# Attention with clustered masks and two feed-forward layers: the first two heads in another order, two heads assigned as a pair, a second bank for transpositions

## The chip, the cores and the metric

One core of a Trainium2 chip runs the whole program. The metric is device time in microseconds (us) of one execution; less is better. The core has a matrix engine (TensorE, PE below; PEld is its loading of weights), a vector engine (VectorE, DVE), an engine for functions of one input (ScalarE, ACT), GpSimd (POOL) and SyncE (SP), which here only issues DMAs. Each engine works through its instructions in order; semaphores hold an instruction until what it needs from another engine is there. PE writes to PSUM, eight banks, from which DVE and ACT read.

## The reference

Attention over 2 batches x 8 heads, 768 positions, 64 dimensions, with a mask: each query and each key is assigned to the nearest of 16 centroids of its head (largest cosine), and a query sees the keys of its own cluster only. Then two feed-forward layers over the 1536 x 512 result.

```python
q_assign = argmax(einsum('bhsd,hcd->bhsc', q_n, c_n))      # k_assign alike
mask = q_assign[:, :, :, None] == k_assign[:, :, None, :]
scores = where(mask, scale * q @ k.T, -1e9)
attn = exp(scores - max(scores)); attn /= (sum(attn) + 1e-9)
x = (attn @ v) reshaped to [1536, 512]
h = x @ w_in;   x = (h * sigmoid(1.702 * h)) @ w_out        # 512 -> 2048 -> 512
g = x @ w_gate; out = (g * sigmoid(g) * (x @ w_val)) @ w_out2
```

All is float32.

## The kernel before, in words

The 16 heads (2 batches x 8) go one after the other. For a head h, the steps that matter here are:

- `hi_q`, `hi_k` (ACT) and `lo_q`, `lo_k` (DVE or POOL) split queries and keys into a rounded part and the difference. Results lie in `q2(h)` and `k2(h)`, five buffers each, used in turn; inputs come by DMA into four staging buffers (`load_qk`).
- `similar` (line 435): four matmuls of 128x384 give the products of keys and queries with the centroids, into one bank (`sims`). `largest` and `assign` (lines 459 to 504) turn them on DVE into rows that say to which cluster each position belongs: a transposition of 32x32 blocks, an addition, a maximum, a comparison, a weighting, a second maximum, a comparison, a scaling, and two transpositions back (`oT`). For one head these work on 192 columns and the rows are copied into `q2` and `k2` by given engines (line 494). For a pair they work on 384 columns; the first head's rows are copied (line 502), the second's go by DMA (line 504).
- `smax(h, c, n)` (lines 517, 522): a matmul of 128x384 with its own rounded parts, for block c of six and half n of two, and a reduction on DVE to the maximum of each query. Twelve of them, then `mneg` (line 533), then the row of negated maxima, brought into `q2` either by three matmuls and a copy per half (`mrow_at_once`, lines 540, 544) or by one matmul, a copy and a DMA (`mrow`, lines 549 to 552).
- `scores(h, c, n)` (lines 564, 571): two matmuls of 128x384 into one bank (`st`), the second with the cluster rows and the row of maxima, then an exponential on ACT into `p`. Twelve of them.
- `pv(h, c)` (line 580): six products of `p` with the values, six times; `norm` (lines 597 to 599) divides by the sum.
- `to_x` (lines 609 to 616): when a pair of heads is done, three transpositions on PE for each half n, a copy on ACT and a subtraction on DVE give the input of the feed-forward part.

Loops: the scores of head h stand with the maxima of head h + 1 between them; behind them the six products of head h, and among these the row of maxima and the splitting of later heads, and at odd h the assignment of heads h + 3 and h + 4 and `to_x` for the pair finished before. From head 3 on, steps that decode the feed-forward weights (lines 70 to 86) stand among the products too. The first heads have an order of their own, written out ahead of the loop: head 0's maxima stand with warming matmuls (`keep_warm`, line 353), the first half of its scores alone, the second with the first half of head 1's maxima; heads 1, 2 and 3 are assigned one by one, from head 4 on in pairs.

The order of the work is that of the code: the scheduler is told to leave every engine's instructions in the order in which they are written. Where two tiles share memory, a wait is put in. PSUM is in four pools: `ps_m` two banks (maxima), `ps_x` one bank (similarities, the row of `mrow`, transpositions of `to_x`, each third maximum), `ps_o` two banks (products, warming matmuls), `ps_s` three banks (scores, some similarities).

Of the kernel before, what the change touches and what calls it, by code (L numbers as in the profile page):

```python
# [8 lines left out]
F32 = mybir.dt.float32  # L9
# [16 lines left out]
def tile_cluster_attention_two_mlps(ctx: ExitStack, tc: tile.TileContext, qk, v, cen, w1, w2, wg, wv, w3, out):  # L26
    nc = tc.nc
# [6 lines left out]
    SC = S // 128  # L34
    HALF = S // 2
    NH = B * H
# [235 lines left out]
    with ExitStack() as att:  # L272
# [233 lines left out]
        def do(steps):  # L506
            for _ in steps:
                pass
# [94 lines left out]
        def to_x(hp, n):  # L603

            b, j = divmod(hp, H // 2)
            x = xr_t[hp]
            ps = ps_x.tile([128, HALF], F32, tag="x", name="xt")
            for c in range(SC // 2):
                nc.tensor.transpose(
                    out=ps[:, c * 128:(c + 1) * 128],  # L610
                    in_=x[:, n * (SC // 2) + c, :, :].rearrange("p a d -> p (a d)"),
                    identity=ident,
                )
            at = slice(n * HALF, (n + 1) * HALF)
            nc.scalar.copy(xh[b][:, j, at], ps)
            nc.vector.tensor_tensor(
                out=xl[b][:, j, at], in0=ps, in1=xh[b][:, j, at].bitcast(F32), op=ALU.subtract
            )
# [21 lines left out]
        lo_k(2, nc.gpsimd)  # L640
        extra_rows(3)
        load_qk(4)
        for i, (c, n) in enumerate((c, n) for m in range(2) for n in range(2) for c in range(3 * m, 3 * m + 3)):
            smax(0, c, n, *((ps_m, "m"), (ps_m, "m"), (ps_s, "s"), (ps_s, "s"), (ps_s, "s"))[i % 5])
            keep_warm(1)
            if i == 5:
                mneg(0, slice(0, SC // 2))
            if i == 9:
                mrow_at_once(0, 0, ps_o, "o")
        mneg(0, slice(SC // 2, SC))  # L650
        sims = similar([1])
        for c in range(SC):
            scores(0, c, 0)
        do(largest([1], sims))
        do(assign([1], (nc.vector.tensor_copy, nc.gpsimd.tensor_copy)))
        lo_q(2, nc.gpsimd)
        mrow_at_once(0, 1, ps_o, "o")
        maxima = list(steps)
        for i in range(SC):
            scores(0, i, 1)  # L660
            smax(1, *maxima[i], *((ps_m, "m"), (ps_m, "m"), (ps_x, "x"))[i % 3])
        hi_k(3)
        hi_q(3)
        lo_k(3, nc.gpsimd)
# [1 line left out]
        for t in v_t[1:]:  # L666
            nc.gpsimd.memset(t[:, :, D:D + 1], 1.0)
        extra_rows(4)

        for h in range(NH):
            more, ahead = h + 1 < NH, h + 4 < NH
            if h > 0:
                maxima = list(steps) if more else []
            for step in steps if h else ():
                scores(h, *step)
                if maxima:
                    next_smax(h + 1, maxima)
            if h == 0:  # L680
                load_qk(5)
            if ahead and h > 0:
                hi_q(h + 4)
            if 0 < h < NH - 1:
                mneg(h + 1)
            if h % 2 == 0 and 0 < h < NH - 3:
                do(assign([h + 2, h + 3]))
# [5 lines left out]
            for c in range(SC):  # L693
                pv(h, c)
                if more and c == 0:
                    if h > 0:
                        mrow(h + 1)
                    load_v(h + 1)
                    if ahead:
                        if h > 0:  # L700
                            hi_k(h + 4)
                            lo_q(h + 4)
                            lo_k(h + 4)
                        if h + 6 < NH:
                            load_qk(h + 6)
                        if h + 5 == NH:
                            qk1_stack.close()
                            stage_stack.close()
                            for to, t in zip((xh, xl), new_x(pool(ctx, "x1", 1, side="right"), 1)):
                                to.append(t)  # L710
                            w_pools.append(pool(ctx, "wd0", MID, side="right"))
                if h == 0:
                    if c == 0:
                        sims = similar([2])
                    if c < 3:
                        for i in (2 * c, 2 * c + 1):
                            smax(1, *maxima[SC + i], *((ps_m, "m"), (ps_s, "s"), (ps_m, "m"), (ps_s, "s"))[i % 4])
                    if c == 3:
                        mneg(1)
                        mrow(1, ps_o, "o")  # L720
                        hi_k(4)
                        hi_q(4)
                        do(largest([2], sims))
                        do(assign([2], (nc.scalar.copy, nc.vector.tensor_copy)))
                        lo_k(4)
                        lo_q(4)
                if h == 1 and c == 1:
                    do(largest([3], similar([3])))
                    do(assign([3]))
                if h > 0 and c == 0:  # L730
                    norm(h - 1)
                if h == NH - 1 and c > 0:
                    run([], [[("1", 0)], [("1", 1), ("2", 0)], [("1", 2)], [("2", 1)], []][c - 1], 0)
# [1 line left out]
                if h == 1 and c == 4:  # L735
                    fetch_to(2)
                if h % 2:
                    if c == 2 and ahead:
                        do(largest([h + 3, h + 4], similar([h + 3, h + 4], ps_s, "s")))
                    if c in (3, 4) and h > 2:  # L740
                        to_x((h - 3) // 2, c - 3)
# [74 lines left out]
```

## Time and profile before

| | |
|---|---|
| median of three runs | 855.67 us (855.47 to 855.67) |
| profiled execution | 855.47 us, span of the profile 853.5 us |
| PE busy | 837.7 us, 98% |
| DVE, ACT, POOL busy | 594.0, 432.9, 27.7 us |
| attention part | up to about 285 us |
| heads' scores begin | head 1: 38.97 us; head 2: 60.91 us; head 3: 77.02 us |

The profile is one execution, recorded by the chip. Busy time is time in which an engine works on an instruction; a matmul's duration includes its run through the array, so matmuls that follow each other overlap, and 0.34 us of duration come each 0.17 to 0.18 us. The time that an engine waits stands in brackets behind the instruction that ended the wait, with the instruction that released it. The clock column is the mean share of full speed that PE's clock was granted; 1.00 is 2.4 GHz, 0.50 is 1.2 GHz.

### The profile page before, as it was taken

Reading aid. Unit: us, or ns where it says so; the run is one execution under the profiler, and the core shown is the slowest. Engines: PE = TensorE matmul, PEld = TensorE weight load, DVE = VectorE, ACT = ScalarE, POOL = GpSimd, SP = SyncE. Lnnn points to the kernel's source line nnn. Section 1 sums busy time; section 2 is a strip of 40 time slices with the busy share of each in tenths; the row PEclk is TensorE's granted clock in tenths of the full one; section 3 lists DMA queues with packets and bytes.
Section 4 is the critical chain, followed back from the end, with each engine's and each line's share of the span. In section 5 each row is a group of like instructions: output and inputs, shape, how many; then the busy total and the mean of one; then the engine's idle time right before and its main releaser. Section 6 shows DMA issues by size and latency. Waiting matters only on the chain.

```text
span 853.5 us, 12841 instructions
## 1 busy us (share of the span) xinstructions
PE 837.7 (98%) x5034; PEld 752.4 (88%) x5034; DVE 594.0 (70%) x1147; ACT 432.9 (51%) x819; POOL 27.7 (3%) x43
## 2 busy tenths in 40 slices
PE   8899999999999999999999999999999999999998
PEld 6789999999999888888888888888888888888886
DVE  8788988988975488888877676787664344433433
ACT  6657667668565365565655454554432233322322
POOL 8400000000000000000000000000000000000000
PEclk9989999999999999999999999999999999999999
DMA  6121231230132033333222222222200010000001
GB/s 123 27 78 34 81 83 34 58 82 15 40 93 60 26 96 103 116 107 121 76 99 75 75 75 99 64 86 74 74 1 1 1 49 25 1 1 1 1 1 74
DMA packets 26191, 49.71 MB, mean 58 GB/s; under 512 B 14522, under 2 KB 14612, under 8 KB 26132
## 3 DMA queue, kind: packets, MB, share of 16 engines
q1 hardware_dynamic: 25188, 47.14, 18.8%
q10 hardware_dynamic: 944, 1.77, 0.6%
q8 instruction: 39, 0.64, 0.3%
q14 instruction: 20, 0.16, 0.1%
HBM read 45.12 MB, written 3.15 MB: 57 GB/s over the span
## 4 chain that ended last, share of the span: by engine, by line
PE 87%; DVE 9%; ACT 2%; issue 1%; DMA 1%; POOL 0%; SPq 0%; DVEq 0%; ACTq 0%; POOLq 0%
PE h L156 39%; PE a L156 27%; PE pv L580 9%; PE st L564 7%; PE smax L517 4%; DVE nm L522 1%; ACT q L321 1%; DVE q L330 1%; DVE k L336 1%; DVE T L462 1%; DVE T L459 1%; DVE T L472 1%; DVE mx L470 1%; DVE T L474 1%; DVE oT L491 1%
## 5 line engine op out<-in xcount | busy, mean ns | idle before, releaser
L156 PE MATMUL h<-xh,sp 128*128 128x512 f32 (+1 forms) x1280 | 327.2, 337 | 0.1
L156 PEld LDWEIGHTS h<-xh,sp 128*128 128x128 f32 x1280 | 223.2, 189 | 28.5 <-issue 0.3
L156 PE MATMUL h<-xl,sp 128*128 128x256 f32 (+1 forms) x640 | 215.9, 337 | 0.0
L188 DVE SCALAR_TENSOR_TENSOR t<-t,h 128x512 f32<-128x512 f32 x112 | 61.9, 553 | 160.8 <-ACT t L185 160.8
L185 ACT ACTIVATE t<-h 128x512 f32<-128x512 f32 x112 | 54.8, 489 | 204.1 <-PE h L156 204.1
L156 PE MATMUL a<-g,sp 128*128 128x512 f32 (+1 forms) x768 | 139.4, 337 | 0.0
L156 PEld LDWEIGHTS a<-g,sp 128*128 128x128 f32 x768 | 119.9, 189 | 16.7
L580 PEld LDWEIGHTS pv<-v,p 128*128 128x128 f32 x1152 | 134.3, 192 | 0.0
L580 PE MATMUL pv<-v,p 128*128 128x65 f32 x1152 | 134.0, 273 | 0.0
L156 PEld LDWEIGHTS h<-xl,sp 128*128 128x128 f32 x640 | 120.9, 189 | 14.3
L571 ACT ACTIVATE p<-st 128x384 f32<-128x384 f32 x192 | 90.7, 491 | 34.7 <-PE st L564 27.9
L522 DVE TENSOR_REDUCE nm<-smax 128x1 f32<-128x384 f32 x192 | 100.3, 556 | 9.8 <-PE smax L517 9.6
L156 PE MATMUL a<-sp,g 128*128 128x512 f32 x432 | 106.1, 390 | 0.0
L564 PE MATMUL st<-q,k 128*128 128x384 f32 (+1 forms) x384 | 100.5, 349 | 0.2 <-ACT q L544 0.2
L150 DVE TENSOR_TENSOR sp<-w,sp 128x512 fp32r<-128x512 f32 x136 | 92.9, 685 | 5.2 <-ACT sp L149 5.1
L156 PEld LDWEIGHTS a<-sp,g 128*128 128x128 f32 x432 | 79.5, 188 | 15.6
L149 ACT CAST sp<-w 128x512 fp32r<-128x512 f32 x136 | 83.2, 614 | 0.0
L197 DVE TENSOR_TENSOR g<-t,g 128x512 fp32r<-128x512 f32 x112 | 62.1, 554 | 16.1 <-ACT g L194 11.5
L564 PEld LDWEIGHTS st<-q,k 128*128 128x128 f32 (+1 forms) x384 | 70.1, 194 | 2.1 <-ACT p L571 0.6
L517 PE MATMUL smax<-k,q 80*128 80x384 f32 x192 | 66.6, 349 | 4.6 <-DVE nm L522 2.1
L194 ACT CAST g<-t 128x512 fp32r<-128x512 f32 (+1 forms) x48 | 24.8, 516 | 81.2 <-DVE t L193 81.2
L190 ACT CAST g<-t 128x512 fp32r<-128x512 f32 x64 | 33.0, 515 | 31.3 <-DVE t L188 31.3
(98 smaller groups left out, 646.6 us busy)
## 6 DMA issues: line engine op xcount, KB each, us to landing
raw<-in_w SPq DMA_DIRECT2D x44, 512.0 KB
raw<-in_wg SPq DMA_DIRECT2D x12, 512.0 KB
raw<-in_wv SPq DMA_DIRECT2D x12, 512.0 KB
st<-in_qk SPq DMA_DIRECT2D x15, 384.0 KB
v<-in_v SPq DMA_DIRECT2D x16, 192.0 KB
out<-osb ACTq DMA_DIRECT2D x6, 256.0 KB
out<-osb SPq DMA_DIRECT2D x6, 256.0 KB
q<-oT SPq DMA_DIRECT2D x6, 48.0 KB
```

The costliest lines, as they stand in the source:

```text
L149: lambda: nc.scalar.copy(t[:, 0, :], w),
L150: lambda: nc.vector.tensor_tensor(out=t[:, 1, :], in0=w, in1=t[:, 0, :].bitcast(F32), op=ALU.subtract),
L156: nc.tensor.matmul(out=out_ps, lhsT=lhs[a], rhs=rhs[b], start=(start and j == 0), stop=(stop and j == 2), **kw)
L185: nc.scalar.activation(t, hs[0], ACTF.Tanh, scale=tanh_scale)
L188: nc.vector.scalar_tensor_tensor(out=t, in0=t, scalar=1.0, in1=hs[0], op0=ALU.add, op1=ALU.mult)
L190: nc.scalar.copy(g[:, 0, at], t)
L197: nc.vector.tensor_tensor(out=g[:, 1, at], in0=t, in1=g[:, 0, at].bitcast(F32), op=ALU.subtract)
L517: nc.tensor.matmul(out=ps, lhsT=q2(h)[0:ONE + NC, 1, c * 128:(c + 1) * 128], rhs=k2(h)[0:ONE + NC, 1, n * HALF:(n + 1) * HALF],)
L522: nc.vector.tensor_reduce(out=nm_t[h][:, c, n:n + 1], in_=ps, axis=AX.X, op=ALU.max)
L564: nc.tensor.matmul(out=ps, lhsT=k2(h)[0:rows, a, c * 128:(c + 1) * 128], rhs=q2(h)[0:rows, a, at], start=(a == 0), stop=(a == 1),)
L571: nc.scalar.activation(p_t[h, c][:, at], ps, ACTF.Exp, scale=scale)
L580: nc.tensor.matmul(out=pv_t[h][:, i, :], lhsT=p[:, i * 128:(i + 1) * 128], rhs=v_t[h % 3][:, c, :], start=(c == 0 and i == 0), stop=(c == ...
```

## The change

It has four parts. First, head 0's maxima are made block by block: six, then two, then the first row of maxima; the last four stand among the first half of its scores, and the second half of the scores stands alone. Second, head 1's maxima and head 2's move from the scores ahead of them to the products of the head before (`beside`: three maxima behind each of the first four products), so head 1's scores stand alone too. Third, heads 2 and 3 are assigned as a pair, in two pieces: the similarities stand among head 0's products, the second piece behind the eighth of head 1's twelve scores; heads 4 and 5 follow among head 1's products, and their differences go to POOL. Fourth, the second transposition of a finished pair of heads writes a bank of `ps_s` instead of the one bank of `ps_x`, throughout the attention part.

```diff
@@ -604,7 +604,8 @@
 
             b, j = divmod(hp, H // 2)
             x = xr_t[hp]
-            ps = ps_x.tile([128, HALF], F32, tag="x", name="xt")
+            pl, tag = ((ps_x, "x"), (ps_s, "s"))[n]
+            ps = pl.tile([128, 512], F32, tag=tag, name="xt")[:, 0:HALF]
             for c in range(SC // 2):
                 nc.tensor.transpose(
                     out=ps[:, c * 128:(c + 1) * 128],
@@ -640,25 +641,30 @@
         lo_k(2, nc.gpsimd)
         extra_rows(3)
         load_qk(4)
-        for i, (c, n) in enumerate((c, n) for m in range(2) for n in range(2) for c in range(3 * m, 3 * m + 3)):
-            smax(0, c, n, *((ps_m, "m"), (ps_m, "m"), (ps_s, "s"), (ps_s, "s"), (ps_s, "s"))[i % 5])
+        maxima = [(c, n) for m in range(2) for c in range(3 * m, 3 * m + 3) for n in range(2)]
+        for i in range(SC):
+            smax(0, *maxima[i], *((ps_m, "m"), (ps_m, "m"), (ps_s, "s"), (ps_s, "s"), (ps_s, "s"))[i % 5])
             keep_warm(1)
-            if i == 5:
-                mneg(0, slice(0, SC // 2))
-            if i == 9:
-                mrow_at_once(0, 0, ps_o, "o")
-        mneg(0, slice(SC // 2, SC))
-        sims = similar([1])
+        mneg(0, slice(0, SC // 2))
+        for i in (6, 7):
+            smax(0, *maxima[i], ps_m, "m")
+            keep_warm(1)
+        mrow_at_once(0, 0, ps_o, "o")
+
         for c in range(SC):
             scores(0, c, 0)
-        do(largest([1], sims))
-        do(assign([1], (nc.vector.tensor_copy, nc.gpsimd.tensor_copy)))
+            for i in ((8, 9), (10,), (11,), (), (), ())[c]:
+                smax(0, *maxima[i], *((ps_x, "x") if i == 8 else (ps_m, "m")))
+            if c == 2:
+                mneg(0, slice(SC // 2, SC))
+                sims = similar([1])
+                do(largest([1], sims))
+        mrow_at_once(0, 1, ps_o, "o")
+        for c in range(SC):
+            scores(0, c, 1)
+        do(assign([1], (nc.scalar.copy, nc.gpsimd.tensor_copy)))
+
         lo_q(2, nc.gpsimd)
-        mrow_at_once(0, 1, ps_o, "o")
-        maxima = list(steps)
-        for i in range(SC):
-            scores(0, i, 1)
-            smax(1, *maxima[i], *((ps_m, "m"), (ps_m, "m"), (ps_x, "x"))[i % 3])
         hi_k(3)
         hi_q(3)
         lo_k(3, nc.gpsimd)
@@ -666,14 +672,25 @@
         for t in v_t[1:]:
             nc.gpsimd.memset(t[:, :, D:D + 1], 1.0)
         extra_rows(4)
+        hi_k(4)
+        hi_q(4)
+
+        def beside(h, c, banks):
+
+            for i in range(3 * c, 3 * c + 3) if c < 4 else ():
+                smax(h, *steps[i], *banks[i % len(banks)])
 
 
 
         for h in range(NH):
             more, ahead = h + 1 < NH, h + 4 < NH
-            if h > 0:
-                maxima = list(steps) if more else []
-            for step in steps if h else ():
+            maxima = list(steps) if more and h > 1 else []
+            for at, step in enumerate(steps if h else ()):
+                if h == 1 and at == 8:
+                    do(assign([2, 3], (nc.scalar.copy, nc.gpsimd.tensor_copy)))
+                    norm(0)
+                    lo_k(4, nc.gpsimd)
+                    lo_q(4, nc.gpsimd)
                 scores(h, *step)
                 if maxima:
                     next_smax(h + 1, maxima)
@@ -681,7 +698,7 @@
                 load_qk(5)
             if ahead and h > 0:
                 hi_q(h + 4)
-            if 0 < h < NH - 1:
+            if 1 < h < NH - 1:
                 mneg(h + 1)
             if h % 2 == 0 and 0 < h < NH - 3:
                 do(assign([h + 2, h + 3]))
@@ -693,14 +710,14 @@
             for c in range(SC):
                 pv(h, c)
                 if more and c == 0:
-                    if h > 0:
+                    if h > 1:
                         mrow(h + 1)
                     load_v(h + 1)
                     if ahead:
                         if h > 0:
                             hi_k(h + 4)
-                            lo_q(h + 4)
-                            lo_k(h + 4)
+                            lo_q(h + 4, nc.gpsimd if h == 1 else nc.vector)
+                            lo_k(h + 4, nc.gpsimd if h == 1 else nc.vector)
                         if h + 6 < NH:
                             load_qk(h + 6)
                         if h + 5 == NH:
@@ -710,24 +727,23 @@
                                 to.append(t)
                             w_pools.append(pool(ctx, "wd0", MID, side="right"))
                 if h == 0:
-                    if c == 0:
+                    beside(1, c, ((ps_m, "m"), (ps_s, "s")))
+                    if c == 2:
                         sims = similar([2])
-                    if c < 3:
-                        for i in (2 * c, 2 * c + 1):
-                            smax(1, *maxima[SC + i], *((ps_m, "m"), (ps_s, "s"), (ps_m, "m"), (ps_s, "s"))[i % 4])
                     if c == 3:
+                        sims += similar([3], ps_s, "s")
                         mneg(1)
-                        mrow(1, ps_o, "o")
-                        hi_k(4)
-                        hi_q(4)
-                        do(largest([2], sims))
-                        do(assign([2], (nc.scalar.copy, nc.vector.tensor_copy)))
-                        lo_k(4)
-                        lo_q(4)
-                if h == 1 and c == 1:
-                    do(largest([3], similar([3])))
-                    do(assign([3]))
-                if h > 0 and c == 0:
+                        mrow(1)
+                        do(largest([2, 3], sims))
+                if h == 1:
+                    beside(2, c, ((ps_m, "m"), (ps_s, "s")))
+                    if c == 3:
+                        mneg(2)
+                        sims = similar([4], ps_s, "s")
+                    if c == 4:
+                        mrow(2)
+                        do(largest([4, 5], sims + similar([5], ps_s, "s")))
+                if h > 1 and c == 0:
                     norm(h - 1)
                 if h == NH - 1 and c > 0:
                     run([], [[("1", 0)], [("1", 1), ("2", 0)], [("1", 2)], [("2", 1)], []][c - 1], 0)
@@ -735,7 +751,7 @@
                 if h == 1 and c == 4:
                     fetch_to(2)
                 if h % 2:
-                    if c == 2 and ahead:
+                    if c == 2 and ahead and h > 1:
                         do(largest([h + 3, h + 4], similar([h + 3, h + 4], ps_s, "s")))
                     if c in (3, 4) and h > 2:
                         to_x((h - 3) // 2, c - 3)
```

The order on PE at the end of head 0's first scores; `st` are scores, `smax` maxima, `mrow` the row of maxima, `sims` similarities, `k_0` to `k_4` the five buffers of keys. Lines with - stand in the kernel before, with + in the changed one.

```order
 L435 MATMUL sims<-q_1_108,cs 128x384
+L564 MATMUL st<-q_0_107,k_0_112 128x384 x6
+L540 MATMUL mrow_388<-ident,nr 1x128 x3
 L564 MATMUL st<-q_0_107,k_0_112 128x384 x12
-L540 MATMUL mrow_408<-ident,nr 1x128 x3
-L564 MATMUL st<-q_0_107,k_0_112 128x384 x2
-L517 MATMUL smax<-k_1_113,q_1_108 128x384
```

The second row of maxima now stands ahead of all of the second half of the scores, and no maximum of head 1 stands among them.

PE from the last maxima of head 1 to its scores, before:

```order
L517 MATMUL smax<-k_1_113,q_1_108 128x384 x2
L580 MATMUL pv<-v_117,p 128x65 x6
L549 MATMUL mrow<-ident_r,nr 6x128
L580 MATMUL pv<-v_117,p 128x65 x12
L564 MATMUL st<-q_1_108,k_1_113 128x384 x2
L517 MATMUL smax<-k_2_114,q_2_109 128x384
```

and now:

```order
L517 MATMUL smax<-k_1_113,q_1_108 128x384 x3
L435 MATMUL sims<-k_3_115,cs 128x384
L435 MATMUL sims<-q_3_110,cs 128x384
L435 MATMUL sims<-k_3_115,cs 128x384
L435 MATMUL sims<-q_3_110,cs 128x384
L549 MATMUL mrow<-ident_r,nr 6x128
L580 MATMUL pv<-v_117,p 128x65 x12
L564 MATMUL st<-q_1_108,k_1_113 128x384 x24
L580 MATMUL pv<-v_118,p 128x65 x6
L517 MATMUL smax<-k_2_114,q_2_109 128x384 x3
```

The similarities of head 3 stand where a product stood ahead of the row of maxima, and the 24 matmuls of head 1's scores follow each other.

## Rows read from the trace of the kernel before

**Rows 1.** PE on the page: busy time, share of the span, instructions.

```profile
PE 837.7 (98%) x5034; PEld 752.4 (88%) x5034; DVE 594.0 (70%) x1147; ACT 432.9 (51%) x819; POOL 27.7 (3%) x43
```

**Rows 2.** Stages: length, busy PE, PEld, DVE, ACT, POOL; clock, DMA share, GB/s.

```profile
38.97:50.80 11.83, 9.90 (x38) 8.71 (x38) 9.72 (x19) 6.73 (x14) 0.00 (x0) 0.71 0.01 1
50.80:60.90 10.10, 10.10 (x86) 10.10 (x86) 8.38 (x19) 4.96 (x9) 0.00 (x0) 1.00 0.56 146
60.90:69.00 8.10, 6.80 (x38) 6.34 (x38) 7.93 (x18) 6.05 (x13) 0.00 (x0) 1.00 0.06 23
69.00:77.00 8.00, 8.00 (x74) 8.00 (x74) 5.74 (x12) 5.58 (x8) 0.00 (x0) 1.00 0.07 13
```

**Rows 3.** The same table by microsecond, around the low clock.

```profile
40.00:41.00 1.00, 0.33 (x2) 0.33 (x3) 0.93 (x3) 0.51 (x1) 0.00 (x0) 1.00 0.00 0
...
42.00:43.00 1.00, 1.00 (x5) 0.70 (x3) 0.97 (x2) 0.89 (x3) 0.00 (x0) 0.60 0.00 0
...
48.00:49.00 1.00, 1.00 (x4) 1.00 (x4) 0.60 (x2) 0.49 (x1) 0.00 (x0) 0.50 0.00 0
49.00:50.00 1.00, 1.00 (x7) 1.00 (x7) 0.77 (x3) 0.71 (x2) 0.00 (x0) 0.99 0.00 0
```

**Rows 4.** PE's waits, 77 to 290 us: total, times, longest.

```profile
PE xt L609 <- DVE xl L616: 4.3, 5, 0.9
```

**Rows 5.** Timeline, head 0's scores: start, duration, instruction, [idle before it].

```profile
18.18 0.82 PE L540 MATMUL mrow<-ident,nr 128*1 128x128 f32 x6
...
19.03 0.47 ACT L544 CAST q<-mrow 1x384 fp32r<-1x384 f32 x1 [1.52 <-PE mrow L540]
...
21.25 2.46 ACT L571 ACTIVATE p<-st 128x384 f32<-128x384 f32 x6 [1.74 <-PE st L564]
...
25.75 0.44 PE L517 MATMUL smax<-k,q 80*128 80x384 f32 x1 [0.83 <-POOL k L494]
...
29.12 1.45 PE L580 MATMUL pv<-v,p 128*128 128x65 f32 x12
```

**Rows 6.** Timeline, head 1's last maxima and a wait in its scores.

```profile
34.46 0.60 PE L517 MATMUL smax<-k,q 80*128 80x384 f32 x2
...
34.92 1.02 DVE L522 TENSOR_REDUCE nm<-smax 128x1 f32<-128x384 f32 x2 [0.67 <-PE smax L517]
...
40.67 0.45 PE L517 MATMUL smax<-k,q 80*128 80x384 f32 x1 [1.07 <-ACT q L494]
```

**Rows 7.** Timeline, head 2's scores and a pair's assignment on DVE.

```profile
60.33 0.58 DVE L459 STREAM_TRANSPOSE T<-sims 128x384 f32<-128x384 f32 x1
...
63.40 0.56 DVE L474 TENSOR_TENSOR T<-T,wd 128x384 f32<-128x384 f32 x1
63.88 5.89 DVE L522 TENSOR_REDUCE nm<-smax 128x1 f32<-128x384 f32 x12
...
64.48 0.44 PE L517 MATMUL smax<-k,q 80*128 80x384 f32 x1 [1.30 <-DVE nm L522]
...
68.83 0.34 PE L517 MATMUL smax<-k,q 80*128 80x384 f32 x1
...
69.88 0.54 DVE L483 TENSOR_REDUCE mx<-T 128x24 f32<-128x384 f32 x1
...
71.64 1.16 DVE L491 STREAM_TRANSPOSE oT<-T 64x384 f32<-64x384 f32 x2
```

**Rows 8.** Timeline, a difference, a copy, a row's DMA.

```profile
26.77 1.84 POOL L330 TENSOR_TENSOR q<-st,q 64x768 fp32r<-64x768 f32 x1
...
72.89 0.83 ACT L502 CAST q<-oT 16x768 fp32r<-16x768 f32 x1 [1.86 <-DVE oT L491]
...
74.88 0.74 SPq L552 DMA_DIRECT2D q<-row  x1
```

**Rows 9.** Timeline behind a second transposition, head 5 to head 6.

```profile
126.41 0.55 DVE L616 TENSOR_TENSOR xl<-xt,xh 128x384 fp32r<-128x384 f32 x1
...
127.22 4.82 DVE L522 TENSOR_REDUCE nm<-smax 128x1 f32<-128x384 f32 x9 [0.26 <-PE smax L517]
```

## The prediction

> **What bounds the kernel now.** I read the page first: TensorE (PE) is busy for 98% of the span [rows 1]. So time is won only where PE waits, or where its clock is low. The table of busy time by stage comes next: head 1's scores, 38.97 to 50.80, keep PE busy for 9.90 of 11.83 us at a mean granted clock of 0.71, and head 2's scores for 6.80 of 8.10 us [rows 2]. The table by microsecond shows what the clock did: PE was busy for 0.33 us between 40 and 41, the granted clock was 0.60 in 42 to 43 (so it fell to 0.50, which is 1.2 GHz, at 42.2), and it was 0.99 in 49 to 50: 6.8 us at the lower level [rows 3]. Last come PE's waits after 77 us: a single line, five waits of the transposition of a finished pair of heads, 4.3 us in all [rows 4]. These three places are what the change touches; the feed-forward part keeps its order and has no wait of PE, so what is won ahead of it should come out whole at the end.
>
> **Head 0's scores.** Before, the maxima of head 1 stood among the second half of head 0's scores and had to wait for the assignment of head 1: 0.83 us at 25.75; the products began at 29.12 [rows 5]. Now the first row of maxima is made after eight maxima, two pairs (a maximum and a warming product) earlier, so 18.18 becomes about 17.7; with its 0.82 and the copy's 0.47 [rows 5] the first scores run at 19.1. Six score pairs, four late maxima and head 1's similarities are 20 matmuls of 128x384 at 0.18 (24 of them stand between 64.48 and 68.83 [rows 7]), 3.6: 22.7. The second row and its copy, 0.82 + 0.47 and 0.1 of hand-overs, bring 24.1, and six pairs at the pace of the exponentials, 2.46 / 6 = 0.41, let PE go at about 26.2. The products start 2.9 us earlier. The assignment's chain on VectorE (DVE) runs beside this; its copies, now on ScalarE (ACT) behind the last exponential, end at about 27.5 and 28.0, and the first half is wanted at 27.5, when the first product of 1.34 is through (a sixth of the 8.0 us of head 2's products [rows 2]).
>
> **Head 0's products.** They take 8.0 us, the row of maxima included. Beside them now stand all 12 maxima of head 1 (12 x 0.18 = 2.1) and two similarities (8 x 0.18 = 1.4). A wait is added that the trace doesn't show: the row of head 1's maxima now goes to the one bank of its pool, which head 2's similarities hold until DVE has transposed them, and no product stands between the last maxima and that row. The reductions start 0.46 us after the first of such matmuls and take 0.51 each [rows 6]: 0.46 + 3 x 0.51 + 0.1 for the negation + 0.58 for the transposition [rows 7] = 2.7, of which the last three maxima and the second similarity fill 1.2. PE stands still for 1.5 us, at about 35.1 to 36.6, with two products and head 1's scores queued behind. 26.2 + 8.0 + 2.1 + 1.4 + 1.5 = 39.2: head 1's scores start 0.2 us later than before. Nothing is won yet.
>
> **Head 1's scores** now stand alone. Their 24 matmuls are 4.3 us, but 12 exponentials at 0.41 and a copy of 0.83 [rows 8] among them bound the stage: 0.6 to the first, eight exponentials, the copy, one more to free a bank, and the last pair, 0.6 + 3.3 + 0.83 + 0.41 + 0.4 = 5.6, against 11.83. The copy needs the assignment of heads 2 and 3. As a pair that takes 3.6 us from the first transposition to the last weighting and 2.9 from there to the transposed rows [rows 7]: 36.0 + 6.5 = 42.5, before the eighth exponential ends. End: 44.8.
>
> **Head 1's products.** 8.0 + 2.1 + 1.4 = 11.5 against 10.10, end 56.3. The differences of heads 4 and 5 move to GpSimd (POOL), 1.84 each [rows 8]: if it begins them at 44, 1.5 us behind the transposed rows, four end at 51.4, and the similarities that need the last start at 54.2. That is the cover, 2.8 us. The row of head 2's maxima goes by DMA: issued at 74.88 [rows 8], it was there when head 3's scores began at 77.0, the end of the last stage of [rows 2], 2.1 us; here there are about 1.8, so 0.3 may be late.
>
> **Head 2's scores.** Before, DVE came to the maxima at 63.88, 3 us into the stage, after two assignments, and PE waited 1.30 [rows 7]. Now one part of a chain is left: from the second similarity's end, 55.1, its transposition and four steps are 2.8 us, so the reductions start at 57.9, about 0.5 after the first maximum is ready. The fourth maximum waits 0.3; end 62.9, 6.6 us against 8.10, the late row included. Head 2's products stay at 8.0: head 3 starts at 70.9 against 77.0, a gain of 6.1.
>
> **Second bank.** The second transposition of a pair waited some 0.86 for DVE's subtraction of the first, five times [rows 4]. It now writes a bank of the scores' pool. DVE itself is not faster: its chain ended with the second subtraction at 126.96 [rows 9], and the first maximum of the next head, 0.86 earlier, then waits 0.6 for it. Three banks for maxima cover that. The bank taken leaves two for the next six scores; a bank's turn is then two matmuls, 0.18 + 0.44, and an exponential of 0.41 to 0.55, in all 1.03 to 1.17, for two steps of 0.54: some 0.17 lost. Bounds: 0 and 0.86 each; I take 0.69 x 5 - 0.17 (the sixth time, where nothing was to be won) = 3.3, near the upper end, since DVE's reductions of 0.49 catch up with PE's steps of 0.54.
>
> **The clock.** PE had stood still for 1.07 us before 40.67 [rows 6], and the clock fell at 42.2. Here stands a wait of 1.5 us, so I expect a fall 1.5 us after its end again, at about 38. If it lasts the same 6.8 us, head 0's last product loses 1.1, and seven score pairs take 0.70 in place of 0.41, 2.0, less the copy of 0.83 that then lies beside: 2.3. Bounds: 0 without a fall, 3.4 for 6.8 us of work that PE alone bounds. I take 2.0, near the 2.3. The Trainium skill, "TensorE: Matmul & The Clock Gate", section "HAM oscillation — how this bites in real kernels", ties the fall to gaps longer than any wait here; by that rule there is none, and the sum is that of the first rival. The trace disagrees with it: the clock was 0.50 after a wait of 1.07 us [rows 3, 6].
>
> **Sum.** The profiled execution took 855.47 us (span 853.5), as the lowest of the three runs, whose median is 855.67. 855.47 - 6.1 - 3.3 + 2.0 = 848.1; I say 848.0.
>
> The Trainium skill, "SBUF — State Buffer", section "Who interferes with whom", speaks against the move to POOL: a DVE instruction with two SBUF inputs and a POOL instruction that reads SBUF block each other for a whole instruction. No run here shows such a pair at once. By my order POOL is through at 51.4 and DVE's next such step comes at 54; were POOL 3 us later, it would cost up to 1.84, and the sum would be 849.9.
>
> **Rivals.** (1) The clock does not fall: 855.47 - 9.4 = 846.0. For it: in head 2's scores PE waited 1.30 [rows 7] and the stage's mean clock stayed 1.00 [rows 2]. Against it: [rows 3]. (2) The second bank gives nothing: DVE, which still makes both subtractions in its old order, is late by as much as PE is early, and two banks hold the scores up. Then 848.0 + 3.3 = 851.3. For it: DVE goes from the subtraction to the maxima with 0.26 us between [rows 9]. Against it: its 12 reductions take 5.89 us where PE's steps take 6.5 [rows 7]. (3) Slower: the clock falls after the new wait and stays at 1.2 GHz through head 1's scores and products, since the scores alone leave PE waiting on ACT. All PE work from 38 to 56 then takes twice as long, less the 1.4 that ACT bounds: some +16, 846.0 + 16 = 862. It decides from 9.4 us of PE work at the lower clock on. For it: the low stretch before held for 6.8 us. Against it: that ended while scores and maxima ran.
>
> **How the numbers follow.** Forecast, 0.48; (1) 0.30; (2) 0.13, all lesser gains of the bank with it; (3) 0.05; nothing of what is described happens, 0.04. The forecast's own range is 846.5 to 850; (1) asks for 845.2 at the lower end, and most of (2) ends below 852. Range 845.2 to 852. What a measurement can tell from no change is 0.2%, 1.7 us: faster is below 854.0. Faster 0.90 (forecast, (1), nearly all of (2)), same 0.05, slower 0.05.
>
> **What would show it.** Right: products of head 0 from about 26 us; a wait of PE of some 1.5 us on DVE's transposition just before the row of head 1's maxima; head 1's scores in 5.6 us, or 7 to 8 with a low clock; head 3's scores from 71 to 73; no wait left at the transpositions, and 0.5 to 0.86 us won at each of five. Wrong: head 1's scores as long as before, a low clock beyond 46 us, similarities that wait on POOL near 54 us, or scores of the heads behind a transposition waiting on ACT for more than 0.3 us.

## The result and the profile after

The changed kernel takes 847.21 us (median of 4 runs, 847.06 to 847.29) against 855.57 for the kernel before beside it (4 runs, 854.77 to 855.67): a ratio of 0.9898, 95% interval 0.9886 to 0.9911. The profiled execution took 847.29 us, its span is 845.5 (853.5 before).

The page's first line, against [rows 1]. PE is busy for 1.3 us less than before, in a span shorter by 8.0. POOL has 7.7 us more, the copies and differences that moved there.

```profile
PE 836.4 (99%) x5030; PEld 748.7 (89%) x5030; DVE 583.8 (69%) x1131; ACT 431.2 (51%) x816; POOL 35.4 (4%) x48
```

PE's longest waits behind the start of the program (who waits, on whom, total, times, longest). The five waits of a transposition [rows 4] are gone. New are one wait of the row of head 1's maxima and, in head 1's scores, one for an exponential.

```profile
PE mrow L549 <- DVE T L459: 1.2, 1, 1.2
PE st L564 <- ACT p L571: 0.7, 1, 0.7
PE sims L435 <- DVE q L330: 0.5, 1, 0.5
PE st L564 <- ACT q L544: 0.4, 2, 0.2
```

The kernel before had three lines of maxima that waited in the first heads; of these, two waits of 0.2 us are left.

```profile
PE smax L517 <- DVE nm L522: 2.1, 2, 1.3
PE smax L517 <- ACT q L494: 1.3, 2, 1.1
PE smax L517 <- POOL k L494: 1.0, 2, 0.8
```

The table by stage that answers to [rows 2]: head 1's scores, head 1's products, head 2's scores, head 2's products. Columns: length, busy time of PE, PEld, DVE, ACT and POOL, PE's granted clock, DMA. Head 1's scores last 5.86 us at a clock of 1.00, where before 11.83 were spent at 0.71. Head 3's scores, which end the table, begin at 72.12; before it was 77.02.

```profile
39.98:45.84 5.86, 5.11 (x26) 3.83 (x26) 3.82 (x9) 5.17 (x12) 2.44 (x2) 1.00 0.09 18
45.84:57.37 11.53, 11.53 (x95) 11.53 (x94) 7.94 (x18) 3.86 (x6) 5.64 (x4) 1.00 0.22 53
57.37:64.11 6.74, 6.74 (x39) 6.41 (x39) 6.67 (x14) 5.26 (x11) 0.00 (x0) 1.00 0.46 156
64.11:72.12 8.01, 8.01 (x74) 8.01 (x74) 5.68 (x12) 5.44 (x8) 0.00 (x0) 1.00 0.08 15
```

The microseconds in which PE was least busy there, against [rows 3]: PE alone, then its clock. In 36 to 37 it worked for 0.06 us, and the clock stayed at 1.00, there and in every stretch shown after it.

```profile
36.00:37.00 1.00, 0.06 (x1) 1.00 0.00 0
37.00:38.00 1.00, 0.72 (x7) 1.00 0.00 0
44.00:45.00 1.00, 0.64 (x4) 1.00 0.26 49
45.00:46.00 1.00, 0.61 (x4) 1.00 0.30 60
```

Head 0's scores, in the timeline, against [rows 5]: the first row of maxima, the second, the last six exponentials, the first product, 2.2 us earlier than before.

```profile
18.07 0.81 PE L540 MATMUL mrow<-ident,nr 128*1 128x128 f32 x6
...
23.32 0.81 PE L540 MATMUL mrow<-ident,nr 128*1 128x128 f32 x6
...
25.17 2.46 ACT L571 ACTIVATE p<-st 128x384 f32<-128x384 f32 x6 [0.53 <-PE st L564]
...
26.94 1.45 PE L580 MATMUL pv<-v,p 128*128 128x65 f32 x12
```

The new wait, against [rows 6]: DVE reduces the last three maxima, negates (nr), transposes the similarities (T); only then is the bank free that the row needs.

```profile
35.05 1.49 DVE L522 TENSOR_REDUCE nm<-smax 128x1 f32<-128x384 f32 x3 [1.08 <-PE smax L517]
...
36.56 0.17 DVE L533 TENSOR_REDUCE nr<-nm 128x6 fp32r<-128x12 f32 x1
36.65 0.57 DVE L459 STREAM_TRANSPOSE T<-sims 128x384 f32<-128x384 f32 x1
...
37.27 0.23 PE L549 MATMUL mrow<-ident_r,nr 128*6 128x128 f32 x1 [1.22 <-DVE T L459]
```

From head 3 on, PE's starts of the scores tell what the second bank gives. From head 3 to head 15 they lie 189.42 us apart before and 186.15 after: 3.27 won. The lines are the first scores of these two heads, before and then after:

```profile
77.02 0.60 PE L564 MATMUL st<-q,k 128*128 128x384 f32 x2
266.44 0.77 PE L564 MATMUL st<-q,k 128*128 128x384 f32 x3
...
72.12 0.60 PE L564 MATMUL st<-q,k 128*128 128x384 f32 x2
258.27 0.95 PE L564 MATMUL st<-q,k 128*128 128x384 f32 x4
```

The step from an odd head to the next one, with two transpositions in it, fell from 17.54 to 16.41 (heads 3 and 4); the step after it grew from 14.45 to 14.89. The front, up to head 3, gave 4.90.

### The profile page after: what moved, and what is told of

Its sections match the earlier page's. It is cut to its first block, busy times and chain, and to the rows that moved or that the text cites. A ratio compares the mean times of both kernels' runs of the same rounds, so it can differ in the third digit from the quotient of the medians.

```text
span 845.5 us, 12830 instructions
## 1 busy us (share of the span) xinstructions
PE 836.4 (99%) x5030; PEld 748.7 (89%) x5030; DVE 583.8 (69%) x1131; ACT 431.2 (51%) x816; POOL 35.4 (4%) x48
## 4 chain that ended last, share of the span: by engine, by line
PE 94%; DVE 4%; ACT 1%; issue 0%; DMA 0%; ACTq 0%; DVEq 0%; SPq 0%
PE h L156 40%; PE a L156 28%; PE pv L580 13%; PE st L564 8%; PE smax L517 4%; DVE nm L522 1%; PE sims L435 1%; PE warm L353 1%; PE xt L610 0%; DMA q<-oT 0%; DVE q L330 0%; DVE k L336 0%; DVE oT L491 0%; DVE T L459 0%; PE mrow L540 0%
## 5 line engine op out<-in xcount | busy, mean ns | idle before, releaser
L522 DVE TENSOR_REDUCE nm<-smax 128x1 f32<-128x384 f32 x192 | 98.3, 554 | 12.9 <-PE smax L517 12.8
L564 PEld LDWEIGHTS st<-q,k 128*128 128x128 f32 (+1 forms) x384 | 67.1, 190 | 7.1 <-ACT p L571 4.0
L197 DVE TENSOR_TENSOR g<-t,g 128x512 fp32r<-128x512 f32 x112 | 61.9, 553 | 16.1 <-ACT g L194 11.5
L517 PE MATMUL smax<-k,q 80*128 80x384 f32 x192 | 63.4, 345 | 0.6 <-DVE nm L522 0.2
```

The source lines that it names most:

```text
L197: nc.vector.tensor_tensor(out=g[:, 1, at], in0=t, in1=g[:, 0, at].bitcast(F32), op=ALU.subtract)
L517: nc.tensor.matmul(out=ps, lhsT=q2(h)[0:ONE + NC, 1, c * 128:(c + 1) * 128], rhs=k2(h)[0:ONE + NC, 1, n * HALF:(n + 1) * HALF],)
L522: nc.vector.tensor_reduce(out=nm_t[h][:, c, n:n + 1], in_=ps, axis=AX.X, op=ALU.max)
L564: nc.tensor.matmul(out=ps, lhsT=k2(h)[0:rows, a, c * 128:(c + 1) * 128], rhs=q2(h)[0:rows, a, at], start=(a == 0), stop=(a == 1),)
```

## Experiments

The kernels ran in three groups, each beside the kernel before on one chip: the bank, `bank_of_products` and `four_beside` first (before: median 856.77 us, 18 runs), then `warm_in_wait`, the copies, `all_three` and `longer_wait` (856.38, 17 runs), then `warm_three` and `one_transposition` (855.93, 20 runs). Ratios are to these. A ratio is not the quotient of the two medians, since the runs of the kernel before spread widely: its 55 runs lie between 854.6 and 864.2 us.

**The second bank, undone and alone.** `one_bank` is the changed kernel with both transpositions in one bank again; `bank_alone` gives the kernel before the second bank and nothing else.

```diff
 # one_bank
-            pl, tag = ((ps_x, "x"), (ps_s, "s"))[n]
-            ps = pl.tile([128, 512], F32, tag=tag, name="xt")[:, 0:HALF]
+            ps = ps_x.tile([128, HALF], F32, tag="x", name="xt")
 # bank_alone: the same lines, the other way, in the kernel before
```

> The changed kernel with both transpositions of a pair in the one bank of ps_x again; the rest of the change stays. Theory (the bank is worth what heads 3 to 12 gained in the trace, 8.15 - 4.90 = 3.25 us): 850.5 us, five waits of PE on the subtraction, 4.3 us. Rival (the new order of the first heads moves VectorE's work so that the waits would be gone anyway): 847.2, no such waits.

> The kernel before with the second bank for transpositions alone. Theory: 855.6 - 3.25 = 852.3 us, the first heads as before, the clock low from 42 to 49 us. Rival (bank worth nothing without the new order): 855.6.

`one_bank` took 850.52 us (ratio 0.9919, 0.9887 to 0.9951), 3.3 more than the changed kernel, as the theory said, and its trace has the old line of waits back:

```profile
PE xt L609 <- DVE xl L616: 4.2, 5, 0.9
```

So 3.3 us belong to the bank when the rest of the change is there. `bank_alone` took 853.61 us (0.9966, 0.9934 to 0.9998), 1.3 above the theory's 852.3. But the theory counted from 855.6; the kernel before had a median of 856.77 beside it, and from there the gain is 3.2, as forecast. So the two parts are independent here. Its steps from head 3 on are those of the changed kernel (16.31 and 14.86); what differs from the profile of the kernel before lies ahead of them. The rows (length, PE busy, clock) show two stretches at the lower clock, 1.2 GHz, where [rows 3] have one: in head 0's scores and in head 1's.

```profile
26.00:32.00 6.00, 5.81 (x28) 0.72 0.24 68
44.00:52.00 8.00, 6.78 (x24) 0.57 0.01 2
```

The first of these stretches follows a wait of 0.82 us and one of 0.19 in head 0's scores; the kernel before has the same two waits (the longer one in [rows 5]), but no low clock there in the execution that was profiled. So the same order of work brings the clock down in one execution and not in another. Each run comes with its mean granted clock, and the 18 runs of before beside this kernel line up on it: 855.0 to 855.8 us at 0.996, 857.2 to 857.3 at 0.993 and 0.994, 862.8 at 0.983 to 0.984. A straight line through them meets a clock of 1.00 at 853.2 us. That figure is an extrapolation; the runs with warming products below test it.

**A bank of the products for the second transposition.** The scores of the next head lose 0.44 us in the changed kernel, since they are left with two banks for six steps. This edit gives them the third one back.

```diff
-            pl, tag = ((ps_x, "x"), (ps_s, "s"))[n]
+            pl, tag = ((ps_x, "x"), (ps_o, "o"))[n]
```

> The changed kernel with the second transposition in the pool of the products (two banks, one free there) instead of the scores' pool. Theory (the scores of heads 4, 6, 8, 10 and 12 lose 0.4 us each because two banks are left to the first six of them): 5 x 0.4 = 2.0 less, 845.2 us, score steps of 0.53 instead of 0.63. Rival (VectorE, still at the second subtraction, holds up the maxima instead): 847.2.

Measured 846.16 us (0.9862, 0.9828 to 0.9895): 1.05 won, between the two. The step behind a transposition became 14.59 to 14.70, not 14.45. The timeline at that place shows what took over, DVE's second subtraction (xl) and the maximum (smax) that waits for the reductions (nm) queued behind it:

```profile
120.61 0.55 DVE L617 TENSOR_TENSOR xl<-xt,xh 128x384 fp32r<-128x384 f32 x1
...
121.68 0.19 PEld L517 LDWEIGHTS smax<-k,q 80*128 80x128 f32 x1 [0.27 <-DVE nm L522]
```

So of the 0.44 about half is the bank (0.2 us at each of five steps, 1.05 in all), and the rest is DVE, whose chain the change made no shorter.

**Head 1's maxima four at a time.** They then end behind head 0's third product, and two more products lie between them and their row.

```diff
-        def beside(h, c, banks):
+        def beside(h, c, banks, per=3):
...
-            for i in range(3 * c, 3 * c + 3) if c < 4 else ():
+            for i in range(per * c, per * c + per) if per * c < 12 else ():
...
-                    beside(1, c, ((ps_m, "m"), (ps_s, "s")))
+                    beside(1, c, ((ps_m, "m"), (ps_s, "s")), 4)
```

> The changed kernel with head 1's maxima four at a time behind the first three products instead of three behind the first four. Theory (the 1.22 us that PE waits ahead of the row of head 1's maxima are on the path): wait gone, head 1's scores from 38.8 instead of 39.98, 846.0 us. Rival (the path then goes through the assignment of heads 2 and 3, whose copy stands among head 1's scores): 847.2.

Measured 845.68 us (0.9853, 0.9816 to 0.9890): 1.5 won, where the theory had 1.2. The line `mrow <- DVE T` is gone from the waits, and head 1's scores begin at 38.63 instead of 39.98. So the new wait was a cost by itself: in the changed kernel's profile no fall of the clock stands behind it.

**A warming product in the wait of before.** If the wait of 1.07 us in head 1's scores [rows 6] brings the clock down, filling it should keep the clock up.

```diff
                 scores(h, *step)
+                if h == 1 and step == (0, 0):
+                    keep_warm(5)
```

> Kernel before, with five warming products of 128x512 (about 0.21 us each) put where TensorE stood still for 1.07 us in head 1's scores; nothing else moves. Theory (that wait brings the clock down): no granted clock under 0.9 between 42 and 50 us, and 853.2 us, which is where the runs of the kernel before point when their times are drawn against their mean granted clock (583 us for a clock lower by 1, 853.2 at 1.00). Rival (what follows the wait brings it down, the slow start of the stage): the clock falls as before and the time is that of the kernel before run beside it, 855 to 857.

By time this decided nothing: 854.93 us, ratio 1.0003 (0.9974 to 1.0032). The trace says more. In head 1's scores the clock stayed at 1.00, though PE still waited for 1.23 us at 45.7. But in this execution it had already fallen in head 0's scores, as in `bank_alone`, where the wait was not filled and the clock fell a second time. That is one execution of each, and the clock differs from one to the next, so this speaks for the theory and does not show it.

```profile
26.00:32.00 6.00, 5.81 (x28) 0.72 0.29 68
42.00:50.00 8.00, 6.74 (x35) 1.00 0.01 2
```

Of its 12 runs two had a mean clock of 1.00, and these took 853.09 and 853.37 us, where the line through the runs of before had pointed. The other ten ran at 0.984 to 0.998 and took 854.5 to 863.9.

**Warming products in three waits of before.** `keep_warm` can now also go on writing a tile that it is given.

```diff
-        def keep_warm(n):
+        def keep_warm(n, ps=None):
...
             scores(0, i, 1)
+            if i == 0:
+                keep_warm(2)
+                keep_warm(2)
...
                 scores(h, *step)
+                if h == 1 and step in (steps[0], steps[2]):
+                    if step == steps[0]:
+                        warm = ps_o.tile([128, 512], F32, tag="o", name="warm")
+                    keep_warm(5, warm)
```

> Kernel before, with warming products where TensorE stood still three times: four of them (0.21 us each) in head 0's scores (0.83 us), five each after head 1's first and third pair of scores (1.07 and 0.83 to 1.23 us). Nothing else moves. Theory (those waits are the only reason for the low clock, and the low clock costs what the runs drawn against their clock say): mean clock 0.999 to 1.0 in nearly all runs and a median of 853.2 us, 2.4 below the kernel before. So of the front's 4.9 us half would be clock. Rival (the low clock comes from elsewhere, or the lost time is the waits themselves): clocks of 0.983 to 0.997 as before, 855 to 857 us.

Measured 853.28 us, all 12 runs between 853.11 and 853.42 with a mean clock of 0.999 or 1.0; ratio 0.9947 (0.9922 to 0.9972). None of the 55 runs of the kernel before had a mean clock above 0.998. Head 3's scores begin at 74.92 us, against 77.02 before and 72.12 after the change. This splits the front's 4.9 us: 2.1 of them was the low clock, and 2.8 (74.92 to 72.12) is what the new order saves apart from it. These 2.8 are waits, which warming products only fill, and four warming products fewer (PE's 5034 instructions in the page's first line became 5030). The same stretch in `warm_three` (columns as in the table by stage), the start of head 3's scores, and a wait that this kernel keeps, in head 2's scores:

```profile
42.00:50.00 8.00, 7.94 (x49) 7.41 (x47) 7.58 (x15) 5.81 (x13) 0.00 (x0) 1.00 0.01 3
...
74.92 0.60 PE L565 MATMUL st<-q,k 128*128 128x384 f32 x2
...
PE smax L518 <- DVE nm L523: 1.3, 1, 1.3
```

Behind that last wait of 1.3 us the clock stayed up in the profile, and by their mean clock in all 12 runs. So the length of a wait alone does not decide.

**The new wait made longer.** Two transpositions of the same similarities, with outputs that nobody reads, stand ahead of the one that PE waits for; in `one_transposition` it is one (`range(1 ...)`).

```diff
             T = T_t[hs[0]] = am_p.tile([128, HALF], F32, tag="T", name="T")
+            for _ in range(2 if hs == [2, 3] else 0):
+                U = am_p.tile([128, HALF], F32, tag="U", name="U")
+                nc.vector.transpose(out=U, in_=pss[0])
             for j, ps in enumerate(pss):
```

> The changed kernel with two more transpositions of the same similarities on DVE (0.58 us each, their output unused) ahead of the one that TensorE waits for before the row of head 1's maxima: the wait grows from 1.22 to 2.4 us. Theory (a wait brings the clock down when it is long enough, and 1.22 us in these surroundings was not): granted clock of 0.5 somewhere between 38 and 50 us and 847.2 + 1.2 + 2.4 = 850.8 us. Rival (it isn't the length, the work behind a wait decides): clock 1.00 throughout and 848.4 us.

> The changed kernel with one more transposition of 0.58 us ahead of the one that TensorE waits for: a wait of 1.75 us, between 1.22 (mean clock lower in 6 of 22 runs of the kernels that have it) and 2.3 (in 5 of 5). Theory (the longer one wait, the more often the clock falls after it): some runs at 847.8 us and a clock of 0.999 to 1.0, some at 850.4 and 0.995 to 0.997, more than half of them the latter. Rival (what decides is something else than this wait): all at 847.8.

`longer_wait` took 851.10 us (0.9942, 0.9929 to 0.9954), `one_transposition` 850.13 (0.9904, 0.9870 to 0.9939; one of nine runs at a clock of 1.0, with 847.61). In both profiles the clock falls behind the wait. In `longer_wait` by PE's rows:

```profile
36.00:37.00 1.00, 0.00 (x0) 1.00 0.00 0
37.00:38.00 1.00, 0.00 (x0) 1.00 0.00 0
38.00:39.00 1.00, 0.77 (x7) 0.92 0.00 0
39.00:40.00 1.00, 1.00 (x7) 0.50 0.00 0
...
44.00:45.00 1.00, 1.00 (x5) 0.50 0.00 0
45.00:46.00 1.00, 1.00 (x6) 0.67 0.26 49
```

From 0.92 and 0.67 the low stretch runs from 38.84 to 45.66, 6.8 us as before the change. Of the 3.9 us that `longer_wait` lost, 1.1 is the longer wait (2.3 against 1.22), and the 2.8 that are left go to the clock. In `one_transposition` the run without a fall and the six runs at 0.995 and 0.996 that took 850.0 to 850.6 lie 2.4 to 3.0 apart. Counted over the changed kernel and those made from it, by their wait ahead of that row:

| wait ahead of the row | kernels | runs with a mean clock of 0.998 or less |
|---|---|---|
| none | four_beside, all_three | 0 of 10 |
| 1.22 us | changed kernel 0 of 4, one_bank 2 of 7, bank_of_products 1 of 6, copies_on_pool 3 of 5 | 6 of 22 |
| 1.7 us | one_transposition | 8 of 9 |
| 2.3 us | longer_wait | 5 of 5 |

So at this place the clock does fall after a wait, the more often the longer it is, and the wait that the change brought lies where it seldom does. The kernels ran on several chips, but the order holds on the one that had three of these lengths: none 0 of 4 (`all_three`), 1.22 us 3 of 5 (`copies_on_pool`), 2.3 us 5 of 5. A mean clock does not tell where in a run the clock fell; only the two profiles show it behind this wait. What decides in a single run isn't settled: the kernels of the second line have the same order around the wait.

**Both copies on POOL, and the three edits together.**

```diff
-                    do(assign([2, 3], (nc.scalar.copy, nc.gpsimd.tensor_copy)))
+                    do(assign([2, 3], (nc.gpsimd.tensor_copy, nc.gpsimd.tensor_copy)))
```

> The changed kernel, with both copies of heads 2 and 3's transposed rows on GpSimd (POOL) in place of one on ScalarE (ACT) and one on POOL. Theory (the exponentials bound head 1's scores, and the copy of 0.83 us stands among them): head 1's scores shorter by 0.75, 846.5 us. Rival (POOL's second copy comes 0.8 us later, and so do the differences behind it, until head 2's scores or the similarities wait for them): 847.2 us, with a wait of some 0.8 us on POOL in head 1's products or head 2's scores.

> The changed kernel with the three edits that were tried alone: the second half of a transposition in a bank of the products, head 1's maxima four at a time behind head 0's first three products, both copies on POOL. Theory (three separate waits, so the gains add): 847.2 - 1.05 - 1.5 - 0.75 = 843.9 us. Rival (the assignment of heads 2 and 3, which still starts with the similarities behind head 0's third product, becomes what head 1's scores or products wait for): 844.6 to 845.4, with a wait on POOL or DVE between 40 and 50 us.

`copies_on_pool`: 847.70 us (0.9897, 0.9881 to 0.9912), by the median no gain. Its trace has the gain that the theory named: the wait `st <- ACT p` is gone, no wait on POOL came in its place, and the step from head 1's scores to head 2's is 16.45 us instead of 17.39. Two of its five runs took 846.32 and 846.33 us at a clock of 0.999 and 1.0; the other three had a lower one, perhaps behind the 1.22 us wait that this kernel keeps; no profile of such a run shows it. With that wait gone as well, `all_three` took 844.08 us, 843.84 to 844.16, ratio 0.9854 (0.9839 to 0.9869): 3.1 us under the changed kernel where the expectation's three gains add up to 3.3. It is the fastest version here. The longest of PE's waits that are left in it, behind the start:

```profile
PE sims L435 <- DVE q L330: 0.5, 1, 0.5
PE sims L435 <- DVE k L336: 0.4, 1, 0.4
PE st L564 <- ACT q L544: 0.4, 2, 0.2
```

## Why the prediction was right, and where it was wrong

The sum of 848.0 lies 0.8 above what was measured. That it came so close is luck in part, because two errors of opposite sign met in it: a clock term of 2.0 that did not come, and a front that gave 1.2 less.

| step | forecast | measured |
|---|---|---|
| first, second row of head 0's maxima | 17.7, 22.7 | 18.07, 23.32 |
| head 0's products from | 26.2 | 26.94 |
| wait ahead of the row of head 1's maxima | 1.5 | 1.22 |
| head 1's scores from, lasting | 39.2, 5.6 | 39.98, 5.86 |
| head 1's products last | 11.5 | 11.53 |
| head 2's scores last | 6.6 | 6.74 |
| head 3's scores from (front's gain) | 70.9 (6.1) | 72.12 (4.90) |
| second bank | 3.3 | 3.27 |
| clock | +2.0 | 0 |

**Head 0's scores: mis-sized by 0.74.** The order came out as told, but the row was not made at 17.7: the last of the eight maxima ahead of it waited 0.22 us for DVE's reductions, and the first pair with the maxima waited 0.18 for the copy of the row. The matmuls were counted; of the hand-overs between engines 0.1 was. Head 1's scores (+0.26) are of the same kind: their last pair waited 0.75 us for an exponential behind the copy, a wait that the sum had, and what it lacked is small steps between PE and ACT. For head 2's scores (+0.14) the cause stays open.

**The new wait: right.** It stands where it was put, on DVE's transposition just ahead of the row, 0.3 shorter. That head 1's scores start no earlier than before, so that nothing is won until then, was right too (39.98 against 38.99; 0.2 later was forecast), and so was where the gain comes: a stage of 5.86 us in place of 11.83.

**POOL: right.** Its four differences were through at 51.66 (forecast 51.4), and the similarities that need the last ran at 55.36 without a wait:

```profile
49.85 1.81 POOL L336 TENSOR_TENSOR k<-st,k 64x768 fp32r<-64x768 f32 x1
```

The Trainium skill's rule on POOL and DVE ("SBUF — State Buffer", "Who interferes with whom") had nothing to act on: DVE had no instruction with two SBUF inputs between 44 and 52 us. No run here shows such a pair. The row that was to come 0.3 late did not: PE has no wait at the start of head 2's scores.

**Second bank: right in sum, wrong in its parts.** Won were 1.06 to 1.13 us at each of five transpositions, not 0.86: between the two transpositions of a pair lie 1.62 us now and 2.64 in `one_bank`, 1.02 less, of which the wait's row tells 0.86. Lost were 0.38 to 0.52 behind each of the five, not 0.17, and nothing behind the sixth: four steps of 0.63 in place of 0.53, with two banks in turn, as the starts of PE's score pairs show.

```profile
120.33 0.51 PE L564 MATMUL st<-q,k 128*128 128x384 f32 x2
...
120.96 0.62 PE L564 MATMUL st<-q,k 128*128 128x384 f32 x2
...
121.59 0.51 PE L564 MATMUL st<-q,k 128*128 128x384 f32 x2
...
122.22 0.62 PE L564 MATMUL st<-q,k 128*128 128x384 f32 x2
...
122.85 0.52 PE L564 MATMUL st<-q,k 128*128 128x384 f32 x2
```

The loading of weights shows who holds them up, from 77 us to 270, in the changed kernel and then in `one_bank`: an exponential that still reads the bank.

```profile
PEld st L564 <- ACT p L571: 2.4, 11, 0.3
...
PEld st L564 <- ACT p L571: 0.3, 2, 0.2
```

That is 0.42 us more for each of the five heads behind a transposition. So one of the prediction's own signs of being wrong came: scores waiting on ACT there for more than 0.3 us. The net of 0.65 a transposition is what was forecast (0.69), because the larger gain and the larger loss nearly cancel, and that is luck. The prediction named both effects and the limit behind them (DVE is not faster), and `bank_of_products` confirms that limit.

**The clock: the step that failed.** The prediction read one pair of rows, a wait of 1.07 us and a low clock 1.5 us behind it, as a rule for a single wait: "Here stands a wait of 1.5 us, so I expect a fall". The kernel before had a row against that, 1.30 us without a fall in head 2's scores, and the prediction gave it to a rival. What the runs show instead: the fall differs from run to run, and at this place it comes more often the longer the wait is, in 6 of 22 runs at 1.22 us and 13 of 14 at 1.7 and above. In the kernel before, with waits of 0.83 and 0.20 us in head 0's scores and 1.07 and another of 0.83 (1.23 at full clock) in head 1's, no run of 55 was without it, if a mean clock of 0.998 or less is taken as its sign. The place matters too: the 1.3 us in head 2's scores brought none in 12 runs of `warm_three`. So that none of the four runs of the changed kernel had a fall is in part luck as well: of 18 runs of kernels with the same wait, 6 did. The size was better than the chance: where the fall came (`longer_wait`), it lasted 6.8 us and cost 2.8, against 2.0 for 6.8 us in the forecast. The first rival's condition held, and its 846.0 is off by the front's 1.2.

The Trainium skill's page "TensorE: Matmul & The Clock Gate" has two sections that bear on this. "HAM oscillation — how this bites in real kernels" ties the fall to gaps longer than any of these; the traces of `longer_wait` and `one_transposition` disagree, with falls behind waits of 2.3 and 1.7 us. "A second HAM failure mode: psum-queue depth-cycling" tells of an engine that goes between the two levels because it stands still briefly and often; the waits of the kernel before, several within a few microseconds, are of that kind, and filling them kept the clock up in all 12 runs of `warm_three`.

**What the gain consists of.** On the medians, which come from more than one chip, 855.57 to 847.21 is 8.4 us: 2.3 for the low clock that the old order brought on (to 853.28, `warm_three`; 2.7 against the runs beside it), 2.8 for the waits and warming products that the new order of the first heads saves (to 850.52, `one_bank`), 3.3 for the bank. In the prediction the first of these was hidden in the front's term, since the stage of 11.83 us that it replaced held the low clock.

## What to carry to other kernels

Where the clock is low in a stretch, look for the waits ahead of it and fill them with a product that nobody needs: it costs one line, and if the time falls, that part of a stage's length was clock and not order. A wait that is moved is worth another edit: a bank that an earlier tile still held cost 1.5 us here, and spreading the work ahead of it differently took that away. When a buffer is taken from one user to serve another, price the loss at each turn of the user that gave it, and ask whether the next engine in the chain has become any faster.

## What was not expected of the hardware

The mean granted clock of a run tells its time: 18 runs of one kernel on one chip spread over 7.8 us, and their clocks of 0.983 to 0.996 put them in order to within 0.2 us. The lower level lasted 6.8 us in three profiles (42.2 to 49.0 before, 38.84 to 45.66 in `longer_wait`, 39.66 to 46.48 in `one_transposition`, from its rows below) and about as long in head 1's scores of `bank_alone` (8.00 us at a mean of 0.57). In head 0's scores of `bank_alone` and of `warm_in_wait` it lasted half of that, 3.4 us (6.00 at 0.72). This suggests that runs differ by how many such stretches they have. The slowest runs, at 0.983, must by that figure have spent some 29 us at the lower level (0.017 of 861 us, doubled, since it is half of full speed); this is an estimate, and no profile shows where.

```profile
39.00:40.00 1.00, 1.00 (x10) 0.83 0.01 3
...
46.00:47.00 1.00, 1.00 (x6) 0.76 0.61 140
```
